# Second feed-forward layer: Strassen's seven products on pairs of blocks for the first product, with streamed weights and outputs summed in SBUF

## The chip, the core and the metric

The kernel runs on one core of a Trainium2 chip. The metric is the device time of one execution in microseconds (us). Before the change it is 1731.09 us, the median of three runs (1730.34 to 1733.05).

## What is computed

Linear attention with a norm per head, then two feed-forward layers on 4608 tokens of 512 features with 2048 hidden features. The weights are float64, all else is float32.

```python
kv  = einsum('bhsd,bhse->bhde', k, v)               # 8 batches, 8 heads, 576 tokens, 64 features
o   = einsum('bhsd,bhde->bhse', q, kv)
x   = o / sqrt(mean(o * o, -1) + 1e-6) * g_norm     # then [4608, 512]
h   = x @ w_in1;  y   = (s * relu(h) ** 2 + b) @ w_out1
h   = y @ w_in2;  out = (h * sigmoid(h)) @ w_out2
```

## The kernel before

**Numbers.** A float32 product runs as three passes: each operand is split into hi (rounded by ScalarE, `rnd`) and lo (the difference, `rest`, on VectorE or GpSimd), and hi x hi, hi x lo and lo x hi are summed in PSUM (`mm3`).

**Blocks and units.** The tokens are cut into NB = 9 blocks of T = 512: the first 512 of each of eight batches, and a ninth block of the 64 that are left of each. A unit is one layer, one block and one tile m of 128 hidden features, KF = 16 tiles: `mm1` makes h in PSUM from four slices of x (4 x 3 matmuls), ScalarE takes its activation (L549), ScalarE and VectorE make hi and lo, and `mm2`, LAG2 = 1.6 units later, adds the tile's part to four accumulators of the block, which stay in PSUM over all 16 tiles (4 x 3 matmuls; L605 to L607 in the second layer). At the end of a block `block_out` copies the four accumulators out and stores them: to `y1` in DRAM in the first layer, to the output in the second. `load_x` brings a block of `y1` back as x of the second layer into the one buffer `x32`, and `split_x` splits it.

**Weights.** `decode` turns float64 bits into float32 hi and lo: loads into `raw`, then operations on ScalarE, VectorE and GpSimd (L240 to L270). 32 tiles of both weights stay in SBUF, 4 KB of a partition each, tags `wi0` to `wi15` and `wo0` to `wo15`. The four that are wanted last (`late = order[-LATE:]`: o13, i15, o14, o15) lie in a pool of their own on the other side of SBUF. The second layer's weights are decoded during the first layer, in halves of a tile with three `dw2` buffers, stored to DRAM (`w2_d`, tile `spill`), and loaded into the same 32 tiles in the last block of the first layer (`reload`, L619 to L624), where each tile is free after its last use.

```python
pool = pools["late"] if (kind, m) in late else wp
...
pools["late"] = ctx.enter_context(tc.tile_pool(name="late", bufs=1, side="right"))
```

**Attention** (`attention_pair`, `normalize`, `last_block`) makes x of the next block beside the units of the first layer, two heads at a time, with two buffers each for k and v, their last tokens, and q.

**Order.** `Plan` sets the order of every engine's queue when the kernel is built. An operation has a key, engines with prices, facts that it needs and makes, and buffers that it takes and gives back. The plan goes through time, and an engine takes up the operation that can start first, among equals the one of the lowest key. On the chip the queues run in that order and wait for each other's semaphores. All transfers but four small ones at the start are issued by SP, in the plan's order too. A buffer tag has as many places as `Plan`'s first argument says, one if it isn't named there, as `x32`.

Of the kernel before, what the change touches and what calls it, by code (L numbers as in the profile page):

```python
# [15 lines left out]
class Plan:  # L16
    """A list schedule: the order in which the engines can take up a kernel's operations.

    An operation has a key (the lower, the earlier it is wanted), its engines with their prices, the facts that it
    needs, opens (at its start) and makes, and the buffers that it takes and gives back (after the last of their users).  # L20
    """
# [5 lines left out]
    def __init__(self, room):  # L27
        self.room, self.ops, self.users = room, [], {}
# [6 lines left out]
    def run(self):  # L35
# [21 lines left out]
        def begin(e, op, when):  # L57
            t = max(free[e], when)
            for tag, _ in op[6]:
                s = slots.setdefault(tag, [0.0] * self.room.get(tag, 1))  # L60
                if not s:
                    return None
                t = max(t, min(s))
            return t

        done = 0
        while done < len(self.ops):
# [14 lines left out]
            for tag, _ in op[6]:  # L82
                slots[tag].remove(min(slots[tag]))
# [10 lines left out]
            for b in op[7]:  # L94
                users[b] -= 1
                known[b] = max(known.get(b, 0.0), end)
                if not users[b]:
                    slots[b[0]].append(known[b])
# [10 lines left out]
def kernel(  # L109
# [34 lines left out]
    LAG2 = 1.6  # L144
    LATE = 4
    # exponent bias 1023 - 127 of the float64 words, read with three exponent bits less
# [6 lines left out]
    ap = ctx.enter_context(tc.tile_pool(name="ap", bufs=1))  # L153
# [29 lines left out]
    def dma(dst, src):  # L183
# [4 lines left out]
    w2_d = {(kd, m): dr.tile([P, 2, DM], F32, name=f"w{kd}2_{m}") for kd in "io" for m in range(KF)}  # L188

    plan = Plan({"acc": 4, "h": 2, "at": 2, "kv": 2, "rem": 2, "q": 2, "part": 2, "rms": 2, "gh": 3, "y": 2,  # L190
                 "raw": 4, "dw": 4, "raw2": 2, "dw2": 3})
# [3 lines left out]
    def both(n):  # L195
        """An elementwise operation of two tensors on either engine."""
# [8 lines left out]
    # ---- weights: a tile is 128 of the hidden features, hi and lo; they come in the order of their use  # L205
# [12 lines left out]
    def decode(layer, kind, m, c, width, sfx, key, needs=()):  # L218
        """Float64 bits to float32 hi and lo."""
# [18 lines left out]
        def mag(e):  # L238
            st["w"] = pool().tile([P, width], F32, tag="dw", name="dw", bufs=nbuf[1])
# [6 lines left out]
        def top(e):  # L246
            """The float32 with 20 bits of mantissa, in place of the high words."""
# [5 lines left out]
        def carry(e):  # L253
            """The low words to the float32's last three bits (and what is carried beyond), to the nearest."""
# [3 lines left out]
        def total(e):  # L258
            """The float32's bits, an integer sum."""
            nc.gpsimd.tensor_tensor(u32(st["w"]), st["raw"][:, :, 1], st["raw"][:, :, 0], op=ALU.add)  # L260

        def hi(e):
            if layer == 0:
                t = w_tile(kind, 0, m) if c == 0 else w_t[kind, 0, m]
                st["t"] = t[:, :, ss]
            else:
                st["t"] = pool().tile([P, 2, width], F32R, tag="spill", name="spill")
# [9 lines left out]
        add(act(width), key - 0.5, mag, needs=[f(0)], makes=[f(1)], takes=[dw])  # L277
# [11 lines left out]
        else:  # L289
            spill = ("spill" + sfx, me)  # L290
# [478 lines left out]
```

## Time and profile before

| | |
|---|---|
| median of three runs | 1731.09 us |
| the profiled execution, first to last instruction | 1729.5 us |
| TensorE busy | 1682.0 us, 97%, 7937 matmuls |
| weight loads, VectorE, ScalarE, GpSimd busy | 79%, 36%, 34%, 17% |
| mean granted TensorE clock | 0.990 of 2.4 GHz |
| moved by DMA | 127.16 MB, 74 GB/s in the mean |

Matmuls are pipelined, and a matmul's busy time reaches over the next one's start; its cost in a dense stretch is the distance from start to start. "Idle before" is the time an engine stood still ahead of an instruction, with what released it. A line such as L175 can be a helper's, used for many tiles; the tile's name tells them apart.

### The profile page before, as it was taken

What the parts mean: (1) busy time and instruction counts of PE and PEld (TensorE: products, weight loads), DVE (VectorE), ACT (ScalarE), POOL (GpSimd) and SP (SyncE); (2) the same over time, 40 slices, a digit from 0 to 9 for tenths busy, and PEclk for the clock granted to TensorE, in tenths of its full rate; (3) what the DMA queues carried; (4) which work ended last, traced back from release to release, by engine and by line L of the source; (5) the groups of instructions that cost most, each with busy time, mean ns of one, the idle gap of its engine ahead of it and who ended that gap; (6) DMA issues with size and microseconds to landing.
All of it is one profiled execution on the core that took longest, in us unless ns stands there. A gap on an engine that the chain in (4) does not pass through costs nothing.

```text
span 1729.5 us, 20445 instructions
## 1 busy us (share of the span) xinstructions
PE 1682.0 (97%) x7937; PEld 1370.2 (79%) x7937; DVE 627.7 (36%) x1040; ACT 593.8 (34%) x1110; POOL 293.4 (17%) x282
## 2 busy tenths in 40 slices
PE   8889999999999999999999999999999999999994
PEld 6667788888888888888888888888888888888883
DVE  6999665666743444334321111111111111111110
ACT  4555445454533333332323232323232323232321
POOL 4565343333401010010101010101010101010100
PEclk9989999999999999999999999999999999999997
DMA  9653645555521112010553010101010101010000
GB/s 198 190 165 90 185 130 172 159 160 160 147 66 48 43 29 61 2 49 1 171 195 122 1 49 1 49 1 49 1 49 1 49 1 49 1 49 1 25 1 24
DMA packets 165848, 127.16 MB, mean 74 GB/s; under 512 B 95096, under 2 KB 144248, under 8 KB 164600
## 3 DMA queue, kind: packets, MB, share of 16 engines
q1 hardware_dynamic: 165624, 125.86, 25.0%
q8 instruction: 62, 1.02, 0.3%
q14 instruction: 34, 0.28, 0.1%
q0 software_dynamic: 128, 0.00, 0.0%
HBM read 89.13 MB, written 36.70 MB: 73 GB/s over the span
## 4 chain that ended last, share of the span: by engine, by line
PE 89%; DVE 5%; DMA 2%; issue 1%; SPq 1%; ACT 1%; POOL 0%; DVEq 0%; ACTq 0%
PE h L167 14%; PE h L169 14%; PE h L168 14%; PE acc L605 8%; PE acc L607 8%; PE acc L606 8%; PE acc L167 7%; PE acc L168 7%; PE acc L169 7%; PE kv_ps L371 1%; DVE raw L244 1%; DVE raw L249 1%; SPq L184 1%; DVE raw L256 1%; DMA raw<-in_moe_w_out_dram 1%
## 5 line engine op out<-in xcount | busy, mean ns | idle before, releaser
L549 ACT ACTIVATE g<-h 128x512 f32<-128x512 f32 x288 | 172.1, 598 | 823.2 <-PE h L169 815.0
L168 PE MATMUL h<-xl,wi 128*128 128x512 f32 x1152 | 450.9, 391 | 3.1 <-DVE xl L175 3.1
L169 PE MATMUL h<-xh,wi 128*128 128x512 f32 x1152 | 450.7, 391 | 1.9 <-DVE wi L175 1.9
L167 PE MATMUL h<-xh,wi 128*128 128x512 f32 x1152 | 450.8, 391 | 0.0
L175 DVE TENSOR_TENSOR gl<-g,gh 128x512 fp32r<-128x512 f32 x151 | 110.9, 735 | 652.5 <-ACT gh L172 652.5
L168 PEld LDWEIGHTS h<-xl,wi 128*128 128x128 f32 x1152 | 216.9, 188 | 51.8 <-DVE xl L175 4.8
L169 PEld LDWEIGHTS h<-xh,wi 128*128 128x128 f32 x1152 | 216.8, 188 | 49.6 <-DVE wi L175 3.2
L167 PEld LDWEIGHTS h<-xh,wi 128*128 128x128 f32 x1152 | 217.2, 189 | 46.9
L167 PE MATMUL acc<-gh,wo 128*128 128x512 f32 x576 | 234.7, 407 | 4.2 <-ACT gh L172 3.9
L175 POOL TENSOR_TENSOR xl<-x,xh 128x512 fp32r<-128x512 f32 x63 | 85.1, 1354 | 884.5 <-ACT xh L172 882.0
L168 PE MATMUL acc<-gl,wo 128*128 128x512 f32 x576 | 227.6, 395 | 5.2 <-POOL gl L175 3.2
L169 PE MATMUL acc<-gh,wo 128*128 128x512 f32 x576 | 226.4, 393 | 0.0
L605 PE MATMUL acc<-wo,gh 128*128 128x512 f32 x576 | 224.9, 390 | 0.0
L607 PE MATMUL acc<-wo,gl 128*128 128x512 f32 x576 | 224.8, 390 | 0.0
L606 PE MATMUL acc<-wo,gh 128*128 128x512 f32 x576 | 224.7, 390 | 0.0
L557 DVE SCALAR_TENSOR_TENSOR g<-g,vecs 128x512 f32<-128x512 f32 x128 | 100.9, 788 | 236.8 <-ACT g L549 236.6
L167 PEld LDWEIGHTS acc<-gh,wo 128*128 128x128 f32 x576 | 108.9, 189 | 28.1 <-ACT gh L172 5.6
L168 PEld LDWEIGHTS acc<-gl,wo 128*128 128x128 f32 x576 | 109.0, 189 | 27.7 <-POOL gl L175 4.8
L169 PEld LDWEIGHTS acc<-gh,wo 128*128 128x128 f32 x576 | 108.9, 189 | 23.5
L606 PEld LDWEIGHTS acc<-wo,gh 128*128 128x128 f32 x576 | 108.2, 188 | 23.2
L607 PEld LDWEIGHTS acc<-wo,gl 128*128 128x128 f32 x576 | 108.1, 188 | 23.2
L605 PEld LDWEIGHTS acc<-wo,gh 128*128 128x128 f32 x576 | 108.1, 188 | 22.9
(88 smaller groups left out, 1311.9 us busy)
## 6 DMA issues: line engine op xcount, KB each, us to landing
raw<-in_moe_w_out_dram SPq DMA_DIRECT2D x38, 256.0 KB, 3.2
y<-y SPq DMA_DIRECT2D x36, 256.0 KB, 3.2
x<-y SPq DMA_DIRECT2D x9, 1024.0 KB, 4.8
raw<-in_moe_w_in_dram SPq DMA_DIRECT2D x34, 256.0 KB, 2.8
wi<-spill SPq DMA_DIRECT2D x32, 256.0 KB, 2.5
wo<-spill SPq DMA_DIRECT2D x32, 256.0 KB, 2.5
wi<-wi SPq DMA_DIRECT2D x16, 512.0 KB, 4.2
wo<-wo SPq DMA_DIRECT2D x16, 512.0 KB, 3.7
```

Source lines behind the costliest of these rows:

```text
L167: nc.tensor.matmul(ps, wh, xh, start=first, stop=False)
L168: nc.tensor.matmul(ps, wh, xl, start=False, stop=False)
L169: nc.tensor.matmul(ps, wl, xh, start=False, stop=last)
L175: eng[e].tensor_tensor(lo, src, f32(hi), op=ALU.subtract)
L184: nc.sync.dma_start(out=dst, in_=src)
L244: nc.vector.tensor_scalar(hi, hi, 0x80000000, None, op0=ALU.bitwise_and)
L249: nc.vector.scalar_tensor_tensor(out=hi, in0=u32(st["w"]), scalar=3, in1=hi, op0=ALU.logical_shift_left, op1=ALU.bitwise_or)
L549: nc.scalar.activation(g_t[u], h_t[u], AF.Relu if layer == 0 else AF.Silu)
L557: nc.vector.scalar_tensor_tensor(out=g_t[u], in0=g_t[u], scalar=s_t, in1=g_t[u], op0=ALU.mult, op1=ALU.mult)
L605: nc.tensor.matmul(a_t[d], gh[:, dd], w[:, 0], start=start, stop=False)
L606: nc.tensor.matmul(a_t[d], gh[:, dd], w[:, 1], start=False, stop=False)
L607: nc.tensor.matmul(a_t[d], gl[:, dd], w[:, 0], start=False, stop=stop)
```

## The change

The second layer's first eight blocks are taken as four pairs. For a pair, and for two neighbouring hidden tiles (a step, eight of them: NS), the first product is a 2 x 2 by 2 x 2 product of halves: x is halved over features and blocks, w over features and hidden tiles. Instead of eight half-products it makes seven (Strassen, in Winograd's form) of sums and differences: four sums of weight quarters (made once, in the first layer, by `factors`) and four of x's quarters (`pair_x`, for each pair). The seven collect in three PSUM banks, X, Y and Z, and are brought together by five additions on VectorE. The eight weight factors go to DRAM with their hi and lo and are streamed for each step, as are the second weights. The second product's sum over a step stays in PSUM for two hidden tiles only; the sums over the steps are in SBUF (`y2`), one addition on VectorE for each of eight output tiles of a step. The ninth block runs in units as before, with its weights streamed too. The 32 weight tiles of the first layer become the places of the x factors (14), of w_in's (6) and w_out's (5) streams and of hi and lo of the hidden features (7). Attention has one buffer each for k and v, their last tokens, and q, and the decoding of the second layer has one.

```diff
-    w2_d = {(kd, m): dr.tile([P, 2, DM], F32, ...) for kd in "io" for m in range(KF)}
-    plan = Plan({"acc": 4, "h": 2, "at": 2, "kv": 2, "rem": 2, "q": 2, ..., "raw": 4, "dw": 4, "raw2": 2, "dw2": 3})
+    w2_d = {(kd, j): dr.tile([P, 8, 2, QW], F32, ...) for kd in "io" for j in range(KF // 2)}
+    plan = Plan({"acc": 4, "h": 2, "at": 2, "kv": 1, "rem": 1, "q": 1, ..., "raw": 4, "dw": 4, "raw2": 2, "dw2": 1, "tmp": 8})
...
+    A11, S2, S1, A12, S3, A22, S4, A21 = range(8)
+    def factors(kind, j, key):
...                                        # decode of four quarters into one tile w [P, 8, QW]
+        for o, a, b_, op, needs in (
+            (S1, A21, A22, ALU.add, parts), (S3, A11, A21, ALU.subtract, parts),
+            (S2, S1, A11, ALU.subtract, [("sum", S1) + me]), (S4, A12, S2, ALU.subtract, [("sum", S2) + me]),
+        ):
...
+            add(both(QW), key + 0.6 + 0.01 * o, go, needs=needs, makes=[("sum", o) + me])
+        for g in range(4):
+            sp = ("spill2", me + (g,))
...
+            add(act(2 * QW), key + 0.7 + 0.1 * g, hi, needs=parts + sums, makes=[("fh", g) + me], takes=[sp])
+            add(both(2 * QW), key + 0.72 + 0.1 * g, lo, needs=[("fh", g) + me], makes=[("fl", g) + me], gives=[("dw2", me)])
+            add({"SP": 0.48}, key + 0.74 + 0.1 * g, out_, needs=[("fl", g) + me], makes=[("w2", g) + me], gives=[sp], move=1.46)
...
+    def place(b):
+        tag = plan.place[b]
+        return (pools["late"] if tag in [f"w{kd}{m}" for kd, m in late] else wp).tile([P, 2, DM], F32R, tag=tag, name=b[0])
...
-        if layer == 0 and t == NB - 1:     # reload into the weight tiles
+        if layer:                          # the ninth block's weights, a tile for each m
...
+                    for c in range(2):
+                        dma(f32(tile_)[:, :, c * QW:(c + 1) * QW], w2_d[kind, m // 2][:, quarter_of(kind, m % 2, c)])
...
+    B11, T2, T1, B21, T3, T4, B22 = range(7)
+    X, Y, Z = range(3)
+    BANK = (X, Y, Z, X, Y, Y, Z)
+    def pair_x(tp, kk, key):
+        xb = ("x32", ("pair",) + me)
+        def load(e):
+            t = st["x"] = xp.tile([P, KD, T], F32, tag="x32", name="x32")
+            for h in range(2):
+                dma(t[:, 2 * h:2 * h + 2], y1[2 * tp:2 * tp + 2, :, kk + KH * h].rearrange("n p t -> p n t"))
...
+        sub(T1, ...); sub(T2, ...); sub(T3, ...); sub(T4, ...)     # both(T) each
+        for i in range(7):
+            b_ = (f"xo{i}{kk}", tp)
+            k2 = base(tp) + 4 / 7 * (i + 0.5 * kk) - 1.2
+            add(act(T), k2, hi, needs=..., makes=[("pxh", i) + me], takes=[b_])
+            add(both(T), k2 + 0.02, lo, needs=..., makes=[("xo", i) + me] + ..., gives=[xb, ("xt", me)])
+    def win_loads(tp, j):
+        for g in range(4):
...
+                dma(f32(t)[:, :w], w2_d["i", j][:, 2 * g:2 * g + w])
+    def hidden(tp, j):
+        key = base(tp) + 4 * j
+        read = {3: "x1", 4: "u2", 5: "u3", 6: "h22"}
+        for i in range(7):
+            for kk in range(KH):
...
+                add({"PE": 0.68}, key + 4 / 7 * (i + 0.5 * kk), mm(i, kk),          # three matmuls
+                    needs=[("xo", i, tp, kk), ("wi", tp, j, i // 2)] + before + ([(read[i],) + me] if i in read and kk == 0 else []),
+                    ..., gives=[("win", (tp, j, i // 2))] + [(f"xo{i}{kk}", tp)] * (j == NS - 1))
...
+        add({ACT: 0.59, DVE: 0.69}, k(0), x1, needs=done(0), makes=[("x1",) + me], takes=[tb["x1"]])
+        add({DVE: 0.69}, k(1), plus("a", Y, "x1"), needs=done(1) + [("x1",) + me], makes=[("u2",) + me], takes=[tb["a"]])
+        add({DVE: 0.69}, k(4), plus("b", Y, "x1"), needs=done(4) + [("u2",) + me], makes=[("u3",) + me], takes=[tb["b"]])
+        add({DVE: 0.69}, k(4) + 0.05, plus("b", Z, "b"), needs=done(2) + [("u3",) + me], makes=[("h22",) + me])
+        add({DVE: 0.69}, k(5), plus("c", Y, "x1"), needs=done(5) + [("u3",) + me], makes=[("h21",) + me], ...)
+        add({DVE: 0.69}, k(6), plus("a", Z, "a"), needs=done(6) + [("h22",) + me], makes=[("h12",) + me], gives=[bk[Z]])
...                                        # four times: Silu and hi on ACT, lo on both(T)
+    def wout_loads(tp, j):
...                                        # two tiles of two transfers of 256 KB
+    def outputs(tp, j):
+        for n in range(2):
+            for d in range(KD):
+                tt = n * KD + d
+                key = base(tp) + 4 * j + 4 + LAG3 + 0.5 * tt                        # LAG3 = 0.6
...
+                        nc.vector.tensor_tensor(y2[tp, tt], st["ps"], y2[tp, tt], op=ALU.add)   # a copy where j == 0
...
+                add({"PE": 1.36}, key, mm, needs=..., ..., takes=[acc], gives=...)   # six matmuls
...
-                    decode(1, kind, m, c, DM // 2, "2", KF + 3 + 1.95 * j, needs=[("late",)])
+                factors(kind, j, KF + 3 + 6 * (2 * j + n))
...
+        wanted = [f"xo{i}{kk}" for i in range(7) for kk in range(KH)] + ["win"] * 6 + ["wout"] * 5 + ["g2"] * 7
+        for m in range(KF):
+            for kind in "io":
+                lent_to[f"w{kind}{m}"] = wanted[2 * m + (kind == "o")]
...
+        for pr in range(NPR):
+            for kk in range(KH):
+                pair_x(pr, kk, base(pr) - 12 + 4 * kk)
+            for j in range(NS):
+                win_loads(pr, j); wout_loads(pr, j); hidden(pr, j); outputs(pr, j)
```

## Rows read from the trace of the kernel before

**Rows 1.** The head of the profile page and its first part: busy time, share of the span and instructions of each engine.

```profile
span 1729.5 us, 20445 instructions
PE 1682.0 (97%) x7937; PEld 1370.2 (79%) x7937; DVE 627.7 (36%) x1040; ACT 593.8 (34%) x1110; POOL 293.4 (17%) x282
```

**Rows 2.** Its second part: the span in 40 equal slices, the busy share of each in tenths, and TensorE's granted clock in tenths of full speed.

```profile
PE   8889999999999999999999999999999999999994
PEclk9989999999999999999999999999999999999997
```

**Rows 3.** Busy time of the engines in stretches of the span (from and to, length, then us busy and instructions), the granted clock, the DMA engines' share and GB/s.

```profile
300.00:400.00 100.00, 100.00 (x524) 81.53 (x523) 68.52 (x136) 48.56 (x107) 37.40 (x43) 1.00 0.55 160
...
600.00:700.00 100.00, 100.00 (x509) 81.69 (x508) 41.45 (x65) 34.35 (x65) 10.65 (x8) 1.00 0.15 39
1200.00:1300.00 100.00, 100.00 (x441) 82.44 (x440) 14.32 (x20) 26.11 (x43) 5.17 (x4) 1.00 0.06 21
```

**Rows 4.** The chain that ended last, its share of the span by engine.

```profile
PE 89%; DVE 5%; DMA 2%; issue 1%; SPq 1%; ACT 1%; POOL 0%; DVEq 0%; ACTq 0%
```

**Rows 5.** The timeline of ScalarE: the start of the first activation of successive units, around a block's end in the second layer, and in its last block (start, length, line, tiles; in brackets the idle time before).

```profile
990.37 0.60 ACT L549 ACTIVATE g<-h 128x512 f32<-128x512 f32 x1 [4.18 <-PE h L169]
995.81 0.60 ACT L549 ACTIVATE g<-h 128x512 f32<-128x512 f32 x1 [4.18 <-PE h L169]
1001.40 0.60 ACT L549 ACTIVATE g<-h 128x512 f32<-128x512 f32 x1 [0.70 <-PE h L169]
1006.99 0.60 ACT L549 ACTIVATE g<-h 128x512 f32<-128x512 f32 x1 [3.95 <-PE h L169]
1012.58 0.60 ACT L549 ACTIVATE g<-h 128x512 f32<-128x512 f32 x1 [1.30 <-PE h L169]
1018.05 0.60 ACT L549 ACTIVATE g<-h 128x512 f32<-128x512 f32 x1 [4.21 <-PE h L169]
...
1690.48 0.60 ACT L549 ACTIVATE g<-h 128x512 f32<-128x512 f32 x1 [4.18 <-PE h L169]
...
1695.92 0.60 ACT L549 ACTIVATE g<-h 128x512 f32<-128x512 f32 x1 [4.18 <-PE h L169]
...
1701.51 0.60 ACT L549 ACTIVATE g<-h 128x512 f32<-128x512 f32 x1 [4.33 <-PE h L169]
```

**Rows 6.** Stretches as in rows 3: the first begins in the unit ahead of the slower intervals and ends with the first of them.

```profile
995.00:1001.40 6.40, 6.40 (x29) 5.19 (x28) 0.69 (x1) 3.13 (x5) 3.21 (x3) 1.00 0.00 0
...
1018.05:1023.49 5.44, 5.44 (x25) 4.51 (x24) 0.69 (x1) 1.23 (x3) 0.00 (x0) 1.00 0.00 0
```

**Rows 7.** The timeline of TensorE: the last matmul of the unit whose activation starts at 1690.48 in rows 5.

```profile
1690.05 0.39 PE L169 MATMUL h<-xh,wi 128*128 128x512 f32 x1
```

**Rows 8.** Groups of instructions by line and shape: line, engine, operation, out<-in, count, then busy us and mean ns of one, then idle time before.

```profile
L549 ACT ACTIVATE g<-h 128x512 f32<-128x512 f32 x288 | 172.1, 598 | 823.2 <-PE h L169 815.0 <-POOL gl L175 2.7 <-DVE gl L585 2.4
L175 DVE TENSOR_TENSOR gl<-g,gh 128x512 fp32r<-128x512 f32 x151 | 110.9, 735 | 652.5 <-ACT gh L172 652.5
L172 ACT ACTIVATE gh<-g 128x512 fp32r<-128x512 f32 x160 | 101.0, 631 | 21.4 <-DVE g L560 17.2
L175 POOL TENSOR_TENSOR xl<-x,xh 128x512 fp32r<-128x512 f32 x63 | 85.1, 1354 | 884.5 <-ACT xh L172 882.0
L480 DVE SCALAR_TENSOR_TENSOR x<-o_ps,vecs,inv 128x512 f32<-128x512 f32 x32 | 23.7, 741 | 0.4
L175 DVE TENSOR_TENSOR wo<-dw,wo 128x512 fp32r<-128x512 f32 x9 | 10.4, 1155 | 0.0
```

**Rows 9.** DMA issues: out<-in, queue, count, KB each, median us from issue to landing.

```profile
x<-y SPq DMA_DIRECT2D x9, 1024.0 KB, 4.8
raw<-in_moe_w_in_dram SPq DMA_DIRECT2D x34, 256.0 KB, 2.8
wi<-spill SPq DMA_DIRECT2D x32, 256.0 KB, 2.5
...
wi<-wi SPq DMA_DIRECT2D x16, 512.0 KB, 4.2
```

**Rows 10.** A stretch as in rows 3, in the last block of the first layer, where the second layer's weights are loaded.

```profile
860.00:880.00 20.00, 20.00 (x90) 16.57 (x89) 6.02 (x8) 4.70 (x7) 0.00 (x0) 1.00 0.59 206
```

**Rows 11.** Groups as in rows 8: the steps of the decoding of 256 columns.

```profile
L260 POOL TENSOR_TENSOR dw<-raw 128x256 uint32<-128x256 uint32 x72 | 51.9, 721 | 108.1 <-DVE raw L249 35.3 <-issue 15.4 <-ACT dw L240 14.3
L249 DVE SCALAR_TENSOR_TENSOR raw<-dw,raw 128x256 uint32<-128x256 uint32 x72 | 33.7, 468 | 1.6
L240 ACT ACTIVATE dw<-raw 128x256 f32<-128x256 f32 x72 | 31.2, 433 | 47.0 <-DVE spill L175 16.8 <-POOL spill L175 15.9 <-DMA raw<-in_moe_w_out_dram 11.3
...
L244 DVE TENSOR_SCALAR raw<-raw 128x256 uint32<-128x256 uint32 x72 | 24.9, 346 | 16.5 <-ACT dw L240 16.2
```

**Rows 12.** The instructions that write the tile `spill`: count, shortest, median and longest ns, start of the first and the last in us.

```profile
L172 ACT ACTIVATE spill<-dw x64: 398/417/422, 173.4 to 481.3; 128x256 fp32r<-128x256 f32 x64
```

**Rows 13.** Timelines of TensorE, SP, VectorE and ScalarE: a kv product of the attention, the loads behind it, the last x of that block, and the last unit ahead of the block that uses it.

```profile
515.27 0.69 PE L371 MATMUL kv_ps<-kv 128*64 128x64 f32 x16
...
516.00 0.39 SPq L184 DMA_DIRECT2D kv<-in_k_dram  x1
...
531.74 0.74 DVE L480 SCALAR_TENSOR_TENSOR x<-o_ps,vecs,inv 128x512 f32<-128x512 f32 x1
...
544.99 0.60 ACT L549 ACTIVATE g<-h 128x512 f32<-128x512 f32 x1 [0.77 <-PE h L169]
```

**Rows 14.** The timeline of TensorE: its last matmul.

```profile
1706.67 0.39 PE L607 MATMUL acc<-wo,gl 128*128 128x512 f32 x1
```

**Rows 15.** A stretch as in rows 3, at the start of the first layer.

```profile
100.00:110.00 10.00, 9.01 (x26) 6.93 (x27) 7.20 (x13) 5.23 (x10) 8.63 (x4) 0.66 0.33 104
```

**Rows 16.** The chain that ended last, in order of time: start, us and what, the step at 100 us.

```profile
100.25 4.91 POOL dw L260
```

**Rows 17.** The matmuls of L169, third passes: here those of the first layer's second product, with ns as in rows 12 and the start of the first and the last.

```profile
L169 PE MATMUL acc<-gh,wo x576: 387/389/628, 47.5 to 924.0; 128*128 128x512 f32 x192
```

More of the change, by code (lines that the diff above doesn't have):

```diff
@@ L144 @@
     LAG2 = 1.6
+    LAG3 = 0.6
     LATE = 4
+    QW = DM // 2
+    NS = KF // 2
+    NPR = (NB - 1) // 2
     EXP_SCALE = 2.0 ** -112
@@ L216, in w_tile, with decode @@
         return w_t[kind, layer, m]
-    def decode(layer, kind, m, c, width, sfx, key, needs=()):
+    def decode(layer, kind, m, c, width, sfx, key, needs=(), quarter=None, takes=()):
         me = (layer, kind, m, c)
@@ L262, in hi @@
         def hi(e):
[L263 to L267, printed above, removed]
+            t = w_tile(kind, 0, m) if c == 0 else w_t[kind, 0, m]
+            st["t"] = t[:, :, ss]
             rnd(st["t"][:, 0], st["w"])
@@ L276, in decode @@
         key -= 0.5
-        add(act(width), key - 0.5, mag, needs=[f(0)], makes=[f(1)], takes=[dw])
+        add(act(width), key - 0.5, mag, needs=[f(0)] + ([("dec", 1, 1, kind, m - m % 2, 0)] if layer and not takes else []),
+            makes=[f(1)], takes=[dw] if quarter is None else takes)
         add({DVE: 0.07 + width * 0.52e-3}, key - 0.45, sign, needs=[f(1)], makes=[f(2)])
@@ L288, in decode @@
             add(both(width), key - 0.15, lo, needs=[f(7)], makes=[full], gives=[dw])
-        else:
-            spill = ("spill" + sfx, me)
-            add(act(width), key - 0.2, hi, needs=[f(6)], makes=[f(7)], takes=[spill])
-            add(both(width), key - 0.15, lo, needs=[f(7)], makes=[f(8)], gives=[dw])
-            add({"SP": 0.48}, key - 0.1, lambda e: dma(w2_d[kind, m][:, :, ss], f32(st["t"])), needs=[f(8)],
-                makes=[("w2", kind, m, c)], gives=[spill], move=width * P * 8 / 3.6e5)
+    A11, S2, S1, A12, S3, A22, S4, A21 = range(8)
@@ L515, in hi, with hi2 @@
             rnd(xh, x_t[lb][:, kk])
-        add(act(T), key, hi, needs=[("x32", lb, kk)], makes=[("xh", lb, kk)], takes=[(f"xs{kk}", lb)],
+        def hi2(e):
+            xs[lb, kk] = (lambda t: (t[:, 0], t[:, 1]))(place((f"xo{kk}0", lb)))
+            rnd(xs[lb, kk][0], x_t[lb][:, kk])
+        add(act(T), key, hi2 if lb >= NB else hi, needs=[("x32", lb, kk)], makes=[("xh", lb, kk)], takes=[xs_of(lb, kk)],
             gives=[("x32", lb)])
@@ new lines, in wout_loads, with go @@
+    def wout_loads(tp, j):
+        for f in range(2):
+            b_ = ("wout", (tp, j, f))
+            def go(e, f=f, b_=b_):
+                t = wo_t[tp, j, f] = place(b_)
+                for c in range(2):
+                    dma(f32(t)[:, :, c * QW:(c + 1) * QW], w2_d["o", j][:, quarter_of("o", f, c)])
+            n = (tp * NS + j) * 2 + f
+            add({"SP": 0.96}, base(tp) + 4 * j + 2 * f - 1, go,
+                needs=[("w2", g, "o", j) for g in range(4)] + ([("wouto", n - 1)] if n else []),
+                makes=[("wo", tp, j, f)], opens=[("wouto", n)] + ([("woutend",)] if (tp, j, f) == (NPR - 1, NS - 1, 1) else []),
+                takes=[b_], move=1.46)
```

245 lines of the change are left out of this document (210 added, 35 removed).

## The prediction

> **What bounds the kernel now.** I read the busy times first, then the slices and the stretches, then the chain of waits. TensorE is busy 1682.0 of 1729.5 us [rows 1], every slice from the fourth to the last but one shows 9 for it, and the granted clock is at its full level, 2.4 GHz, from the fifth on [rows 2]. In both layers a stretch of 100 us holds 100.00 us of TensorE work, while VectorE has 41 in the first layer and 14 in the second [rows 3]; the chain is 89% TensorE [rows 4]. So from about 180 us to the last matmul time can only be won by issuing fewer matmuls, or the same ones closer together, and any wait that is put on TensorE is paid in full.
>
> Their spacing is in the first activations of successive units: 5.44 us for 24 matmuls, 0.2267 us each, but 5.59 us three times around each block's end [rows 5]. In the first of those stretches DMA stands at 0.00 and the clock at 1.00 [rows 6], and the last block, which prepares nothing, slows too [rows 5]. What the three intervals share is that tile 15 of the first weight or tiles 13 to 15 of the second are used: these four lie in the pool `late`, at the other end of SBUF. I read 0.15/24 = 0.0062 us more per matmul while an operand lies there; the neighbours with operands elsewhere are slowed with it.
>
> **The change part by part, against the span of 1729.5 us.**
>
> *Matmuls removed.* A step (two hidden tiles, two blocks) had 2 x 2 x 12 = 48 matmuls of the first product; seven products of two halves and three passes make 42. The second product keeps 48. Over 4 pairs and 8 steps 192 matmuls go: 192 x 0.2267 = **-43.5**. A step then takes 90 x 0.2267 = 20.4 us, and layer two has 3264 instead of 3456 matmuls. All have the same shape, so I take the same spacing.
>
> The Trainium skill's "TensorE: Matmul & The Clock Gate", section "Wait — 56ns, not 53.3ns?", gives 215.7 ns for a stream of 512 columns, an estimate of 41.4 us for the 192; [rows 5] show 226.7 here, and the rows decide.
>
> *The slow tiles.* Eight of nine second-layer blocks lose their three slow intervals: -8 x 0.45 = -3.6. But the seven places of `g2`, stationary in the second product, get the tags o12, i13, o13, i14, o14, i15, o15, four of them late. At least 48 x 4/7 = 27 matmuls of a step read one (0.17 us), at most, neighbours included, 6/7 of all 90 (0.48). I take 0.28, nearer the low end, as only one operand is late: 32 x 0.28 = 9.0. Net **+5.4**, bounds +1.8 and +11.8.
>
> "SBUF — State Buffer" of the Trainium skill, "Who interferes with whom", says that PE never waits on anyone for SBUF; by that rule a tile's place costs nothing. The slow intervals do not bear that out as they stand, and no row shows another cause; the time by the rule is a rival below.
>
> *Waits inside a step.* Products 1, 4 and 5 share bank Y, so product 5 may start only when VectorE has read product 4's sum (`read[5]`), and the rest of TensorE's queue, the second product too, stands behind it. From the start of a last matmul to ScalarE's start is 0.43 us, 0.20 after its slot [rows 7]; the add reads PSUM and SBUF, nearest the 741 ns of L480 [rows 8]; waking TensorE lies between 0 and the same 0.20, I take 0.06: 1.0 us. By the keys one group of the previous step's second product (six matmuls, 1.36 us) stands between, so an idle VectorE is in time by 0.36. Its load per step: 13 adds from PSUM (9.6 us) and up to four differences of 0.735 (2.9) = 12.5 of 20.4 us, 61%. An instruction in the way leaves 0.37 on average, beyond 0.36 in some three cases of ten: 0.05 to 0.15 a step. I take 0.1: **+3.2**, bounds 0 and, without the cover, 32 to 56 (below). Products 3, 4 and 6 have one product or more ahead of them. ScalarE's nine operations of about 0.6 (5.5 us) [rows 8] fit.
>
> *Ends of pairs.* `x32` is one buffer. The second half of the next pair's x (1 MB) loads when the first half's last tile, `xo60`, is split, and this waits for product 6 of the last step. From there: split 0.20 + 0.63 + 0.74 to 1.35, load 4.8 [rows 9] and some 0.5 to 1 behind weights and stores in SP's queue, three dependent differences 2.2 and two more operations 1.4: 11 to 13 us. TensorE has 0.7 of that product, two or three groups of step 6 and 10.9 us of step 7's second product: about 14. That covers it, but then the next pair's first step has no second product between products 4 and 5 and waits its 1.0, and VectorE serves 14 splits beside. I take 2 us at each of three ends: **+6**, bounds 0 and 15.
>
> *Entry and last block.* For the first pair tiles become free from m = 0 on in the last block of layer one, 87 us earlier, and x is loaded then; at the entry mm2 trails by 1.6 units. The last block finds its x early, but its weights now come in 1 MB per 5.44 us, 193 GB/s; a stretch before moved 206 at a DMA share of 0.59 [rows 10], with longer rows. A pair step needs 2.9 MB per 20.4 us, 141 GB/s, from eight DMAs that SP issues in about 4 us. Both **+1.5**, bounds 0 and 8. Reloading in the first layer's last block goes, but it lay beside a full TensorE: 0.
>
> *Layer one.* The layer-two decoding now takes one factor buffer of 8 KB and one spill buffer, and writes 33.5 MB instead of 16.8. Four quarters in two raw buffers: about 10 us (433, 346, 468, 721 ns [rows 11] and a second load of 3); sums 2; four splits with a store each, 0.63 + 0.74 to 1.35 + 4 in place: 18 to 21. So 30 to 36 us per factor, 480 to 580 for 16. It ran from 173 to 482 us [rows 12] and will end about 660 to 750; the first pair needs it at about 870, so up to 43 us per factor cost nothing. VectorE then has up to 70% where it has 41, as in the stretch at 300 us, where TensorE is full [rows 3]. Single k, v and q buffers: the next load was issued at 516.00, 0.7 after the kv matmul at 515.27 [rows 13], about when one buffer allows it too, and x had 13 us to spare. **0**, bounds 0 and +5. The first 175 us and the 22 us behind the last matmul stay [rows 14].
>
> Sum: 1729.5 - 43.5 + 5.4 + 3.2 + 6 + 1.5 = 1702.1. The span lies 1.6 under the median of the runs, 1731.1; I carry that: **1704**.
>
> **The rivals.**
>
> *Slower: product 5 waits in every step.* Should the group meant to cover it run before product 4 ends (its `g2` ready early, the next one's late), or should VectorE have two adds or a blocked difference ahead, TensorE stands 1.0 to 2.2 us in each of 32 steps. Besides the other 12.9 us this turns the sign from (43.5 - 12.9)/32 = 0.96 us on. At 1.74 (one add ahead, no cover): 1702.1 - 3.2 + 55.7 + 1.6 = 1756. For it: VectorE carries 61% where it carried 14%, and beside GpSimd a difference took 1155 ns [rows 8]. Against: 1.36 us of cover by the keys. Chance 0.12.
>
> *No change: the ends of pairs stand open.* If step 7's second product is not ready, or stores hold up the load, each end waits 10 us instead of 2, the clock falls (0.66 in the stretch after a wait of 5 us on GpSimd at 100 us [rows 15, 16]), and three ends cost 30: 1728. Against: the order of x is found when the kernel is built. Chance 0.08.
>
> *All second-layer matmuls at the slow spacing.* Now weights and x lie in one pool; if the slow intervals come of where both operands lie to each other, 2880 x 0.0062 = 17.9 in place of 9.0: 1713. Chance 0.13.
>
> *Place costs nothing.* If the slow intervals had a cause that goes with the block's end, the net term is -3.6 instead of +5.4: 1695. Chance 0.15.
>
> *Decoding late*: 50 us per factor would put the pair off by some 110: beyond 1800. The rows give 36 at most; 0.02.
>
> **How the numbers follow.** The likeliest case has the other 0.50: 1704, and 1692 to 1718 when its terms go to the near ends given above (late tiles 1.8 to 11.8, steps 1.6 to 4.8, ends of pairs 0 to 12). The low end, 1689, is the sum with the late term at its low bound and every wait at zero (1729.5 - 43.5 + 1.8 + 1.6); the high end, 1729, takes in the open ends of pairs. Outside lie the slower rival, the late decoding and a few hundredths. Two runs can be told apart from about 0.2%, 3.5 us. Faster: 0.50 + 0.13 + 0.15 + half of 0.08 and a part of the slower rival near its turning point = 0.83; same 0.05; slower 0.12.
>
> **What would show it.** Right: 192 matmuls fewer; a step of 20.4 to 21 us; TensorE over 95% busy from 180 us; idle time before product 5's first matmul under 0.3 us a step, released by VectorE; 1 to 4 us gaps at three ends; last spill before 800 us. Late tiles: spacing 0.233 where `g2` lies there, 0.2267 elsewhere. Wrong: a gap of a microsecond in every step, differences over 1.5 us on VectorE at those places, a falling clock at pair ends, or layer one's last matmul later than 924.0 us [rows 17].

## The result, and the profile after

The changed kernel takes **1691.37 us**, the median of four runs (1690.04 to 1692.20), against 1731.12 for the kernel before beside it: a ratio of 0.9767, 95% interval 0.9753 to 0.9780. It is faster by 39.8 us, 12.6 us more than the 27.1 forecast, and inside the range, near its low end. The profiled execution took 1690.68, its span is 1688.4.

From the page of the changed kernel: its head, the busy times, TensorE's slices with its granted clock, the shares of the chain, and four of the costliest groups (line, engine, operation, out<-in, count, then busy us and mean ns of one, then idle time before).

```profile
span 1688.4 us, 21308 instructions
...
PE 1644.2 (97%) x7748; PEld 1335.4 (79%) x7748; DVE 865.7 (51%) x1336; ACT 647.1 (38%) x1173; POOL 562.9 (33%) x483
...
PE   8789999999999999999999999999999999999995
...
PEclk9989999999999999999999999999999999999998
...
PE 89%; DVE 6%; DMA 1%; issue 1%; ACT 0%; SPq 0%; POOL 0%; DVEq 0%; ACTq 0%; POOLq 0%
...
L833 PE MATMUL hp<-xo,win 128*128 128x512 f32 x1344 | 344.0, 390 | 0.8 <-DVE tmp L858 0.8
L191 POOL TENSOR_TENSOR g<-tmp,g 128x512 fp32r<-128x512 f32 x123 | 159.2, 1295 | 424.0 <-ACT g L188 216.7
...
L937 DVE TENSOR_TENSOR y<-acc,y 128x512 f32<-128x512 f32 x224 | 154.4, 690 | 275.3 <-PE acc L929 273.0
...
L858 DVE TENSOR_TENSOR tmp<-hp,tmp 128x512 f32<-128x512 f32 x160 | 110.4, 691 | 98.8 <-PE hp L833 93.4
```

TensorE is as full as in [rows 1, 2, 4], at the same clock, with 189 fewer matmuls in the records (192 fewer of the product, three more that warm up at the start), and GpSimd nearly twice as busy. L833 is the line of the seven products: TensorE waited 0.8 us there in the whole run. Of the 128 differences for `g`, GpSimd took 123.

Two stretches inside the pairs, columns as in [rows 3]:

```profile
1200.00:1300.00 100.00, 100.00 (x436) 81.57 (x435) 46.02 (x64) 38.82 (x64) 42.23 (x32) 1.00 0.55 180
1300.00:1400.00 100.00, 100.00 (x436) 81.64 (x435) 43.06 (x63) 29.80 (x50) 31.02 (x24) 1.00 0.46 143
```

VectorE has 43 to 46 us in 100, where [rows 3] had 14; the prediction reckoned with 61% of a step. TensorE has no idle time, yet 436 matmuls in 100 us are 0.2294 each, not 0.2267. The timelines tell where that lies. First ScalarE's, the activation that opens each step (three successive steps):

```profile
1166.92 0.60 ACT L877 ACTIVATE tmp<-hp 128x512 f32<-128x512 f32 x1 [7.80 <-PE hp L833]
1187.56 0.60 ACT L877 ACTIVATE tmp<-hp 128x512 f32<-128x512 f32 x1 [7.80 <-PE hp L833]
1208.26 0.60 ACT L877 ACTIVATE tmp<-hp 128x512 f32<-128x512 f32 x1 [7.73 <-PE hp L833]
```

A step takes 20.64 to 20.70 us; 90 x 0.2267 would be 20.40. Then TensorE's timeline: the entry into the first pair, two groups of the second product in one step with those of the first behind them, and the last matmul.

```profile
922.30 0.39 PE L185 MATMUL acc<-gh,wo 128*128 128x512 f32 x1
922.53 2.91 PE L833 MATMUL hp<-xo,win 128*128 128x512 f32 x12
926.23 2.14 PE L833 MATMUL hp<-xo,win 128*128 128x512 f32 x8 [0.79 <-DVE tmp L858]
...
1228.74 0.39 PE L927 MATMUL acc<-wout,g 128*128 128x512 f32 x1
...
1230.14 1.55 PE L833 MATMUL hp<-xo,win 128*128 128x512 f32 x6
1231.53 0.39 PE L927 MATMUL acc<-wout,g 128*128 128x512 f32 x1
...
1232.89 0.84 PE L833 MATMUL hp<-xo,win 128*128 128x512 f32 x3
1233.57 0.39 PE L927 MATMUL acc<-wout,g 128*128 128x512 f32 x1
...
1668.84 0.39 PE L684 MATMUL acc<-wout,gl 128*128 128x512 f32 x1
```

The group of six matmuls of the second product from 1228.74, whose two `g2` tiles both lie in late places, takes 1.40 us to the next start, and the six of the first product behind it 1.39; the group from 1231.53, with no late tile, takes 1.36, and the three behind it 0.68: 0.2267 each. So it is throughout: the 44 groups without a late tile have a median of 1.360 us, the 212 with one or two 1.382 to 1.399. The only wait of this kind that shows is the one at 926.23, in the first step, where no second product stands between products 4 and 5.

From the starts of all 128x512 matmuls in the trace one can set up the whole second layer, counted from layer one's last matmul (L185's `acc<-gh,wo`, at 922.30; 924.0 in [rows 17]). A distance above 0.26 us counts as a gap, what the others have above 0.2267 as slow spacing. The three right columns are kernels of the next section:

| us | before | changed | late moved | all at 480 | before at 480 |
|---|---|---|---|---|---|
| up to layer one's last matmul | 924.0 | 922.3 | 920.6 | 921.7 | 920.7 |
| matmuls behind it | 3435 | 3246 | 3246 | 3246 | 3435 |
| these x 0.2267 | 778.7 | 735.9 | 735.9 | 735.9 | 778.7 |
| slow spacing | 4.0 | 9.2 | 0.2 | 0.2 | -0.1 |
| gaps | 0.0 | 1.5 | 2.9 | 1.6 | 0.0 |
| behind the last matmul | 22.8 | 19.5 | 19.7 | 20.4 | 23.0 |

So the span lost 1.7 us in layer one, 36.2 in layer two and 3.3 behind it, 41.1 in all. Of the 1.5 us of gaps 1.06 are the entry, and 0.45 are two places behind ends of pairs, at 1089 and 1263 us.

The decoding, and the end of layer one: the rows that answer to [rows 12, 17], with count, shortest, median and longest ns, and first and last start.

```profile
L188 ACT ACTIVATE spill<-dw x64: 612/618/635, 187.5 to 720.8; 128x512 fp32r<-128x512 f32 x64
...
L185 PE MATMUL acc<-gh,wo x576: 387/389/628, 48.3 to 922.3; 128*128 128x512 f32 x192
```

The decoding ended at 721 us, within the forecast 660 to 750 and 150 us ahead of its need.

### The profile page after: what moved, and what is told of

Its sections match the earlier page's. It is cut to its first block, busy times and chain, and to the rows that moved or that the text cites. A ratio compares the mean times of both kernels' runs of the same rounds, so it can differ in the third digit from the quotient of the medians.

```text
span 1688.4 us, 21308 instructions
## 1 busy us (share of the span) xinstructions
PE 1644.2 (97%) x7748; PEld 1335.4 (79%) x7748; DVE 865.7 (51%) x1336; ACT 647.1 (38%) x1173; POOL 562.9 (33%) x483
## 4 chain that ended last, share of the span: by engine, by line
PE 89%; DVE 6%; DMA 1%; issue 1%; ACT 0%; SPq 0%; POOL 0%; DVEq 0%; ACTq 0%; POOLq 0%
PE hp L833 18%; PE h L184 8%; PE h L183 8%; PE h L185 8%; PE acc L183 8%; PE acc L184 7%; PE acc L185 7%; PE acc L928 7%; PE acc L929 7%; PE acc L927 7%; PE kv_ps L430 1%; DVE raw L268 1%; DVE raw L275 1%; DVE raw L263 1%; PE acc L684 1%
## 5 line engine op out<-in xcount | busy, mean ns | idle before, releaser
L833 PE MATMUL hp<-xo,win 128*128 128x512 f32 x1344 | 344.0, 390 | 0.8 <-DVE tmp L858 0.8
L191 POOL TENSOR_TENSOR g<-tmp,g 128x512 fp32r<-128x512 f32 x123 | 159.2, 1295 | 424.0 <-ACT g L188 216.7
L833 PEld LDWEIGHTS hp<-xo,win 128*128 128x128 f32 x1344 | 252.0, 188 | 57.6 <-DVE tmp L858 2.1
L937 DVE TENSOR_TENSOR y<-acc,y 128x512 f32<-128x512 f32 x224 | 154.4, 690 | 275.3 <-PE acc L929 273.0
L184 PE MATMUL h<-xl,wi 128*128 128x512 f32 x576 | 227.1, 394 | 2.8 <-DVE xl L191 2.7
L183 PE MATMUL h<-xh,wi 128*128 128x512 f32 x576 | 227.0, 394 | 1.0 <-ACT g L626 0.6
L185 PE MATMUL h<-xh,wi 128*128 128x512 f32 x576 | 226.2, 393 | 0.6 <-DVE wi L191 0.6
L185 PE MATMUL acc<-gh,wo 128*128 128x512 f32 x576 | 226.2, 393 | 0.0
L929 PE MATMUL acc<-wout,g 128*128 128x512 f32 x512 | 201.7, 394 | 0.0
L928 PE MATMUL acc<-wout,g 128*128 128x512 f32 x512 | 201.6, 394 | 0.0
L927 PE MATMUL acc<-wout,g 128*128 128x512 f32 x512 | 201.2, 393 | 0.0
L858 DVE TENSOR_TENSOR tmp<-hp,tmp 128x512 f32<-128x512 f32 x160 | 110.4, 691 | 98.8 <-PE hp L833 93.4
L662 DVE SCALAR_TENSOR_TENSOR gl<-g,vecs,gh 128x512 fp32r<-128x512 f32 x128 | 111.2, 869 | 49.2 <-ACT gh L656 48.2
L183 PEld LDWEIGHTS acc<-gh,wo 128*128 128x128 f32 x576 | 108.7, 189 | 27.0 <-ACT gh L188 5.0
```

What stands on the lines that cost most here:

```text
L183: nc.tensor.matmul(ps, wh, xh, start=first, stop=False)
L184: nc.tensor.matmul(ps, wh, xl, start=False, stop=False)
L185: nc.tensor.matmul(ps, wl, xh, start=False, stop=last)
L191: eng[e].tensor_tensor(lo, src, f32(hi), op=ALU.subtract)
L662: nc.vector.scalar_tensor_tensor(out=st["g"][1], in0=g_t[u], scalar=b_t, in1=f32(st["g"][0]), op0=ALU.add, op1=ALU.subtract)
L833: nc.tensor.matmul(ps, w[:, wn, f_], x_[:, xn], start=first and n == 0, stop=kk == KH - 1 and n == 2, skip_group_check=True)
```

## The experiments

Each theory is about one term of the sum. Only the lines of the edit are shown. Unless a text says otherwise, the kernels compute the same as the changed one.

**1. Where the late tiles lie.** In both kernels the tiles on the left of SBUF that the two layers' matmuls read begin 160 bytes past a multiple of 512, and the four of the pool `late` begin 480 past one. A pad of 320 bytes ahead of that pool makes them alike and leaves the tiles at the far end.

```diff
+    pad = ctx.enter_context(tc.tile_pool(name="pad", bufs=1, side="right"))
+    nc.gpsimd.memset(pad.tile([P, 80], F32, name="pad"), 0.0)
     pools["late"] = ctx.enter_context(tc.tile_pool(name="late", bufs=1, side="right"))
```

> The four late tiles are moved down by 320 bytes of a partition, so that their addresses have the same remainder to 512 bytes (160) as the other 28; nothing else changes. Theory A (the slow spacing comes of the remainder of the address): the matmuls that read one fall from 0.2337 to 0.229 us, some 864 of them in the pairs (-4.1), their neighbours and the nine ends of blocks with tiles 13 to 15 go too (-4 to -5): 8 to 10 us less than the changed kernel's 1691. Theory B (it comes of the far end of SBUF): spacing stays, 1691 within 1. Theory C (it comes of the end of a block, not of the place): stays, too.

Measured: 1680.80 us (1679.19 to 1681.18), 0.9705 of before [0.9691, 0.9720], 10.6 under the changed kernel. ScalarE's timeline of this kernel, the opening of two steps, and TensorE's, one group of the second product:

```profile
1182.10 0.60 ACT L877 ACTIVATE tmp<-hp 128x512 f32<-128x512 f32 x1 [7.63 <-PE hp L833]
1202.50 0.60 ACT L877 ACTIVATE tmp<-hp 128x512 f32<-128x512 f32 x1 [7.63 <-PE hp L833]
```

```profile
1202.24 0.39 PE L927 MATMUL acc<-wout,g 128*128 128x512 f32 x1
...
1203.38 0.39 PE L929 MATMUL acc<-wout,g 128*128 128x512 f32 x1
1203.60 1.52 PE L833 MATMUL hp<-xo,win 128*128 128x512 f32 x6
```

The step is 20.40 us and the group 1.36: every matmul is at 0.2267, with the tiles as far away as before. The far end of SBUF costs nothing, nor does a block's end. Layer one gains too: counted in the same way from 180 us on, its slow spacing is 4.3 us in the changed kernel and 1.1 here.

**2. All tiles at 0.** The left tiles moved by 160 bytes, the late ones by 480.

```diff
-    zeros = const.tile([P, 2 * P], mybir.dt.bfloat16, name="zeros")
+    zeros = const.tile([P, 176], mybir.dt.bfloat16, name="zeros")
+    ...                                  # warm-up matmuls of 176 columns; the pad of above with 120 columns
```

> All 32 tiles, x and the hidden features lie at a remainder of 0 to 512 bytes (the left side 160 bytes lower, paid for by a smaller tile of zeros, so that the warm-up matmuls have 176 columns instead of 256; the late tiles 480 lower). Theory A: late and other tiles have one spacing again, so at least as low as the run with the late tiles moved, 1681 to 1683, and lower if a remainder of 160 also costs something: were the 11 ns between 0.2267 and 0.2157 of that kind, some 6400 matmuls would give another 70 us. Theory B: 1691 within 1.

Measured: 1680.63 (1679.38 to 1682.41), 0.9707 [0.9692, 0.9721]; slow spacing in layer two 0.05 us. Starting at a multiple of 512 gives nothing beyond being alike.

**3. All tiles at 480.** The left tiles alone moved, so that all lie where only the late ones lay. The same edit in the kernel before shows what the old slow intervals cost.

```diff
-    zeros = const.tile([P, 2 * P], mybir.dt.bfloat16, name="zeros")
+    zeros = const.tile([P, 160], mybir.dt.bfloat16, name="zeros")
+    ...                                  # warm-up matmuls of 160 columns
```

> The tile of zeros is 192 bytes smaller (warm-up matmuls of 160 columns), so that the left side moves down by 192 bytes and all operands of the matmuls have the remainder to 512 bytes that the late tiles had, 480. Theory A1 (a remainder of 480 is slow in itself): nearly every matmul at 0.2337 instead of 0.2267 to 0.229, some 5400 more of them slow: about 35 us more than the changed kernel, 1726. Theory A2 (slow is a matmul whose two operands have different remainders): 1681, as with the late tiles moved.

> The same edit in the kernel before. A1: some 6400 matmuls slower by 7 ns: about 40 us more, 1771. A2: the slow intervals at 18 ends of blocks go, 18 x 0.45 to 0.5 = 8 to 9 us less than 1731: 1722. Then the change, measured with all operands at one remainder on both sides, takes off 41 to 42 us instead of 40.

Measured: 1680.59 (1678.60 to 1681.45), 0.9701 [0.9685, 0.9717], and for the kernel before so edited 1724.28 (1723.90 to 1726.43), 0.9959 [0.9945, 0.9974]. ScalarE's timeline of that one, the units at the block's end of [rows 5]:

```profile
992.53 0.60 ACT L549 ACTIVATE g<-h 128x512 f32<-128x512 f32 x1 [4.18 <-PE h L169]
997.97 0.60 ACT L549 ACTIVATE g<-h 128x512 f32<-128x512 f32 x1 [0.67 <-PE h L169]
1003.41 0.60 ACT L549 ACTIVATE g<-h 128x512 f32<-128x512 f32 x1 [3.80 <-PE h L169]
1008.85 0.60 ACT L549 ACTIVATE g<-h 128x512 f32<-128x512 f32 x1 [1.23 <-PE h L169]
```

All intervals are 5.44; the three of 5.59 are gone. So 480 is not slow, and 160 is not: it is slow when operands that are used together differ. The kernel before gains 7 us: 4.1 of slow spacing in layer two, and in layer one, from 180 us on, 3.1 (4.2 to 1.1). Compared alike with alike, the change brings 1724.28 - 1680.59 = 43.7 us, near the 43.5 of the 192 matmuls; its 1.6 us of gaps and its shorter end (20.4 against 23.0) nearly cancel beside that.

The kernel before also tells which operand it is. In layer two's second product the hidden features are stationary and `wo` moves, so there the late tile is the moving operand. With `wo15` the matmuls of L605 to L607 came 0.2337 us apart (mean of 72), and 0.2267 after the edit; the stationary tiles beside them, hidden features and `wi0` or `wi1`, all lie on the left. In the changed kernel the late `g2` is stationary. So either operand can be the one that is off, and two stationary tiles that differ, one after the other, are not needed.

**4. Which difference counts.** The pad of experiment 1 with other sizes: 64, 192 and 256 bytes (16, 48 and 64 columns), which leave the late tiles 256, 128 and 64 bytes off the others.

> A pad of 64 bytes puts the four late tiles at remainder 416 of 512 bytes, 256 from the 160 of all other tiles (320 in the changed kernel as it is). Theory M512, the remainder to 512 bytes counts: the second products with a late g2 stay at about 0.2337 us a matmul, 9 us of slow spacing in the second layer, time about 1691. Theory M256, the remainder to 256 or less counts: all at 0.2267, time about 1681, as in e1_late_moved.

> A pad of 192 bytes: the late tiles at remainder 288, 128 from the other tiles' 160. M128, the remainder to 128 bytes or less counts: 0.2267 everywhere, about 1681. M256 and M512: slow, about 1691. If the price grows with the distance, between the two: 128 is nearer than 320.

> A pad of 256 bytes: the late tiles at remainder 224, 64 from the other tiles' 160. M64, the remainder to 64 bytes counts: this was equal in the changed kernel too (320 is five times 64), so M64 would not explain that kernel's slow matmuls; it is out already and 1691 is expected by M128, M256 and M512. If the price grows with the distance it is the smallest here, some 2 of 9 us: about 1683.

Measured: off by 256 bytes 1681.11 (1680.32 to 1682.11), 0.9710 [0.9695, 0.9724]; by 128 bytes 1691.41 (1690.24 to 1693.86), 0.9771 [0.9756, 0.9785]; by 64 bytes 1690.59 (1689.28 to 1693.63), 0.9762 [0.9745, 0.9778]. Slow spacing in layer two: 0.1, 9.7 and 9.1 us. ScalarE's timelines, two openings of a step, off by 256 and then off by 128:

```profile
1181.80 0.60 ACT L877 ACTIVATE tmp<-hp 128x512 f32<-128x512 f32 x1 [7.63 <-PE hp L833]
1202.20 0.60 ACT L877 ACTIVATE tmp<-hp 128x512 f32<-128x512 f32 x1 [7.63 <-PE hp L833]
```

```profile
1186.71 0.60 ACT L877 ACTIVATE tmp<-hp 128x512 f32<-128x512 f32 x1 [7.78 <-PE hp L833]
1207.48 0.60 ACT L877 ACTIVATE tmp<-hp 128x512 f32<-128x512 f32 x1 [7.78 <-PE hp L833]
```

20.40 against 20.77. Of the differences tried, 0 and 256 are free, and 64, 128 and 320 are not: what has to agree is the remainder to 256 bytes, and the price does not grow with the distance: 64 off costs as much as 320 off. The thought that a small distance is cheap (1683 in the last expectation) failed.

**5. The price of a matmul.** Product 2 of every step is issued twice, 192 matmuls more, so that a step has 96 again. The sums are then those of a doubled product.

```diff
-    nc.tensor.matmul(ps, w[:, wn, f_], x_[:, xn], start=first and n == 0, ...)
+    for again in range(2 if i == 2 else 1):
+        nc.tensor.matmul(ps, w[:, wn, f_], x_[:, xn], start=first and n == 0 and again == 0, ...)
```

> Product 2 of each step is issued twice into its bank (the result is that of a doubled product): six matmuls more in each of 32 steps, 192 in all, so that the first product has its 48 matmuls again, with all else of the change in place. If TensorE's matmuls are the whole story: 192 x 0.2288 = 43.9 us more, 1735, that is 4 us over the kernel before: the other parts of the change then cost about 4 us. If waits were hidden that the additional matmuls now cover, less than 40 us more. If something else set the pace of a step (VectorE, the streamed weights), little more than 1691.

Measured: 1739.56 (1738.16 to 1741.60), 1.0048 of before [1.0031, 1.0065], 48.2 above the changed kernel where 43.9 was expected. TensorE's waits at the seven products in this kernel (us in total, times, longest):

```profile
PE hp L834 <- DVE tmp L859: 5.8, 4, 4.0
```

The span is 49.3 us longer. Gaps are 8.6 us here against 1.5, and 186 of the 192 matmuls lie behind layer one's last: 186 x 0.2267 = 42.2, with the gaps 49.3. The largest gap, 4.1 us, stands in the second pair's first step, ahead of product 6. VectorE's timeline there, the stretch behind the gap (columns as in [rows 3]), and VectorE's timeline at the same place of the changed kernel:

```profile
1102.33 0.68 DVE L859 TENSOR_TENSOR tmp<-hp,tmp 128x512 f32<-128x512 f32 x1
1106.26 1.75 DVE L778 TENSOR_TENSOR x<-x 128x512 f32<-128x512 f32 x1 [3.25 <-DMA x<-y]
1107.93 0.68 DVE L859 TENSOR_TENSOR tmp<-hp,tmp 128x512 f32<-128x512 f32 x1
```

```profile
1108.60:1111.80 3.20, 3.13 (x8) 2.54 (x9) 1.37 (x4) 2.42 (x4) 2.33 (x3) 0.52 1.04 371
```

```profile
1090.94 1.42 DVE L858 TENSOR_TENSOR tmp<-hp,tmp 128x512 f32<-128x512 f32 x2 [1.77 <-PE hp L833]
...
1093.85 0.69 DVE L778 TENSOR_TENSOR x<-x 128x512 f32<-128x512 f32 x1 [0.82 <-DMA x<-y]
```

In this kernel's plan a subtraction for the next pair's x (L778) stands between the two additions that products 5 and 6 wait for. Its load was late, VectorE stood 3.25 us for it, and TensorE 4.0 for the addition behind it. Behind that wait the granted clock was at its lower level, 1.2 GHz (0.52 of 2.4 in the mean of the stretch), and matmuls came 0.43 us apart, 1.5 us more in all. In the changed kernel both additions come first. So the ends of pairs are not safe as such. With the matmuls given back the kernel is slower than before: slow spacing in layer two is 9.1 us against 4.0, and the gaps are 8.6 against none; the shorter end takes back 3.5.

**6. The cover of product 5 taken away.** A step's second product may start only behind the next step's whole first product.

```diff
-    add({"PE": 1.36}, key, mm, needs=[...
+    behind = [("hmo", tp, j + 1, 6, KH - 1)] if j < NS - 1 else []
+    add({"PE": 1.36}, key, mm, needs=behind + [...
```

> A step's second product may start only behind the whole first product of the next step of its pair, so no group of it stands between products 4 and 5. My price: 1.0 us of idle TensorE ahead of product 5 in each step but a few, 28 to 32 us more than 1691, about 1721, and up to 1.74 us a step (1747) if VectorE has an instruction in the way. If the wait is shorter than I priced it: under 20 us more. If product 5 waited for nothing in the changed kernel because its sum is early anyway: 1691.

Measured: 1721.01 (1719.99 to 1721.42), 0.9938 [0.9924, 0.9953], 29.6 above the changed kernel. TensorE's waits, and its timeline inside one step:

```profile
PEld hp L833 <- DVE tmp L858: 37.5, 33, 1.3
...
PE hp L833 <- DVE tmp L858: 23.8, 28, 0.9
```

```profile
1169.08 6.28 PE L833 MATMUL hp<-xo,win 128*128 128x512 f32 x27
1176.22 3.01 PE L833 MATMUL hp<-xo,win 128*128 128x512 f32 x12 [0.85 <-DVE tmp L858]
1179.07 0.40 PE L927 MATMUL acc<-wout,g 128*128 128x512 f32 x1
```

The wait stands between products 4 and 5, and its releaser is VectorE's addition L858. It costs 1.02 us at the first matmul and 0.11 at the next. It is the same in 27 of the 32 steps, 30.4 of the 33.5 us of gaps in layer two. In the changed kernel a group of the previous step's second product, 1.36 us, lies there and hides it.

**7. VectorE's load.** The differences for `g` on VectorE alone, as the prediction had counted them.

```diff
-    add(both(T), kk + 0.15, lo, needs=[("sh",) + q_], makes=[("sl",) + q_], gives=[tb[src]])
+    add(dve(T), kk + 0.15, lo, needs=[("sh",) + q_], makes=[("sl",) + q_], gives=[tb[src]])
```

> The differences (lo) of the hidden features in the pair steps are given to VectorE alone; in the changed kernel 123 of 128 ran on GpSimd. VectorE's load in a pair step rises from about 43% to the 60% that I had reckoned with. My price for such a load: an instruction in the way in some three steps of ten, 0.1 us a step, 3 us more than 1691. Rival: the plan puts them where product 5's sum is not due, and the waits stay under 1 us in all: 1691 within 1.

Measured: 1692.14 (1689.25 to 1692.97), 0.9768 [0.9754, 0.9783], the same as the changed kernel. Its stretches:

```profile
1200.00:1300.00 100.00, 99.86 (x434) 80.89 (x433) 58.65 (x83) 38.15 (x62) 20.98 (x15) 1.00 0.54 178
1300.00:1400.00 100.00, 100.00 (x436) 81.66 (x435) 53.74 (x82) 30.45 (x49) 7.06 (x6) 1.00 0.45 140
```

VectorE has 54 to 59 us in 100 instead of 43 to 46, and the gaps of the whole second layer go from 1.5 to 2.4 us. At this load, VectorE's share does not set the wait.

**8. The end.** In the changed kernel the last five groups of the last step's second product run just ahead of the last six matmuls of the ninth block; two of its four output tiles are done before them. Here the ninth block's second product may start only behind that step.

```diff
-    needs=[("gh", u), ("gl", u)] + ready("o") + ... + [("mm2o", u, d - 1)] * (d > 0),
+    needs=[("gh", u), ("gl", u)] + ready("o") + ... + [("mm2o", u, d - 1)] * (d > 0)
+    + ([("omo", NPR - 1, NS - 1, 2 * KD - 1)] if layer and m == 0 else []),
```

> The ninth block's second product may start only behind the last step's second product of pair 4; in the changed kernel five of its eight groups run just ahead of the last accumulator groups. If the shorter end (19.5 us from the last matmul, 22.8 before) comes of the first two of the four last stores being issued ahead of these groups, the end is 22.8 again and the time 3 us more, about 1694. If it has another cause: 1691.

Measured: 1694.02 (1693.62 to 1695.96), 0.9784 [0.9770, 0.9799]. SP's timeline at the end (issues of the last stores), of the kernel before, of the changed one, and of this one:

```profile
1704.97 9.99 SPq L184 DMA_DIRECT2D out_dram<-x  x4
```

```profile
1660.25 1.83 SPq L200 DMA_DIRECT2D out_dram<-x  x2
...
1669.20 4.73 SPq L200 DMA_DIRECT2D out_dram<-x  x2
```

```profile
1667.16 10.01 SPq L200 DMA_DIRECT2D out_dram<-x  x4
```

Four stores hold SP for 10.0 us, two for 4.7. The end of the span lies 14.4 to 14.6 us behind the last issue in all three (1714.96 to 1729.5, 1673.93 to 1688.4, 1677.17 to 1691.7), so the two early stores are the 3.3 us that the changed kernel gains behind its last matmul; here that stretch is 22.9 again.

## Why the prediction came out as it did

The direction, the main term and the bound were right. The sum gave -27.4 us, the spans differ by -41.1:

| step | forecast | measured | from |
|---|---|---|---|
| 192 matmuls | -43.5 | -43.5 | counted: 189 behind layer one's last matmul, 3 ahead of it, at 0.2267 |
| slow tiles, net | +5.4 | +5.2 | slow spacing 9.2 - 4.0 |
| waits inside a step | +3.2 | 0 | no gap above 0.26 us in a step behind the first, away from the ends of pairs |
| ends of pairs | +6 | +0.45 | gaps at 1089 and 1263 us |
| entry and last block | +1.5 | +1.06 | the gap at 926 us |
| layer one | 0 | -1.0 | 1.7 less 0.7 of the three matmuls |
| behind the last matmul | 0 | -3.3 | experiment 8 |

The measured column sums to -41.1. The 13.7 us between are 8.8 for two waits that did not come, 3.3 for a stretch held to be fixed, and 1.6 for the rest.

**The matmuls** came out as forecast: 192 fewer, and 0.2267 us each wherever all places are alike (a step of 20.40 in experiments 1 and 4). What they took above that is in the table's next line. The estimate by the Trainium skill's "TensorE: Matmul & The Clock Gate", section "Wait — 56ns, not 53.3ns?", 41.4 us from 215.7 ns, was too low: in no kernel here did dense matmuls come closer than 0.2267 us, whatever the addresses.

**The slow tiles** had the right size for a wrong reason. I read from [rows 5] that the far end of SBUF was slow; experiments 1 to 4 show that it is the operands' remainders to 256 bytes differing. The size per matmul had been measured, so it held for the new cause too. My guess of 0.28 us a step stands at 0.24 to 0.30 in the step openings; a late operand slows the neighbours too, as [rows 5] had suggested. The rival "all second-layer matmuls at the slow spacing" named the true cause in its condition, "where both operands lie to each other", but the places of weights and x, all in one pool with tiles of 4 KB, agree with each other, so only the late `g2` paid. The rival "place costs nothing" came nearest in time, 1695 against 1691.4, without being right: with one thing changed, the place, 10.6 us go. That it came near is chance: the late tiles that it left out and the waits that did not come are of one size.

The Trainium skill's "SBUF — State Buffer", section "Who interferes with whom", says that PE never waits on anyone. From it the prediction drew the rival by which a tile's place costs nothing, and that does not hold: a pad that is 64 bytes larger or smaller moved 9 us of TensorE's time in layer two (experiment 4), with no other engine's work changed.

**Waits inside a step**: the failed step is "beyond 0.36 in some three cases of ten". The uncovered price was nearly right, 1.0 forecast and 1.13 in experiment 6. But the share was worked out as if VectorE's work fell at random, and it doesn't. In all 32 steps of the changed kernel the addition starts within 0.50 us of the start of product 4's last matmul, so nothing stands in its way, and behind the first step it ends at least 0.40 us ahead of product 5. In experiment 7, with VectorE at 56%, an instruction stood in its way in three steps, each the first of a pair. The plan orders VectorE's queue with product 5's need in it. The load itself was wrong too, 61% against 45, as I counted four differences on VectorE where GpSimd took 123 of 128. The slower rival rests on the same wait; experiment 6 measures it without the cover at 1721, under the kernel before. The 1756 also asked for an addition in the way, which no run here had in every step.

**Ends of pairs**: the reckoning of 11 to 13 us for the new x against about 14 of cover held: the load was issued at 1072.58, eight groups of the second product ran to 1084.23, and the new half, first used there, was ready. What failed is "the next pair's first step has no second product between products 4 and 5":

```profile
1084.23 6.67 PE L833 MATMUL hp<-xo,win 128*128 128x512 f32 x27
1090.74 0.39 PE L927 MATMUL acc<-wout,g 128*128 128x512 f32 x1
```

The 27 matmuls end with product 4, and the group behind them is the old pair's last; it stands in the same place at the other two ends (1256.27 and 1421.87). So the 1.0 was covered. I had charged as much again for splits in the way; of that 0.34 came at 1089, ahead of product 4, and 0.11 at 1263. Experiment 5 shows that the term was not empty: its late load opens a gap of 4.1 and brings the clock down.

**Layer one**: its last matmul came 1.7 us earlier. Most is there at the start already, 1.5 us by the ninth unit's activation (105.72 before, 104.26 after), and among kernels with the same program up to there that time differs by as much (103.59 in experiment 7, 105.20 in experiment 8); I count it as scatter.

**Behind the last matmul**: "the 22 us behind the last matmul stay" failed. The two layers' ends are now interleaved, and that moves two of the last four stores ahead.

## What to carry to other kernels

Where TensorE is full, count matmuls, price them by their measured spacing, and charge a wait only when its cover, in microseconds of queued work, is shorter than the wait itself; engine load is no probability of a wait in an order that was planned. A late load can still upset that order (experiment 5). Look for a spacing that is not the usual one in the trace of before: here 0.15 us in a few units was an accident of addresses that the change made twice as dear in layer two, and a pad of 64 bytes takes it away. The best version is the changed kernel with all large tiles alike to 256 bytes: 1680.6 to 1681.1 us in four builds (experiments 1 to 4), 0.97 of the kernel before.

## What was not expected of the hardware

float32r matmuls of 128x512 slow down when the addresses of the stationary and the moving tile differ in the remainder to 256 bytes: a step of 90 takes 20.64 to 20.77 us instead of 20.40, with differences of 64, 128 and 320 bytes, and 20.40 with 0 and 256. Three equal places, 0, 160 and 480 past a multiple of 512, gave the same 0.2267. It happens with the stationary tile off (the changed kernel) and with the moving one off (`wo15` in the kernel before, experiment 3). Neighbouring matmuls whose own operands agree are slowed too: six of the first product took 1.39 us instead of 1.36. Why 256, and whether a matmul's moving tile is held against its own stationary tile or the next one's, stays open.
